# Parameter rows ahead of the first weights, and another order around the second half scan, in a kernel of two fused blocks

## The chip, the cores and the metric

The kernel runs on one core of a Trainium2 chip. The metric is the device time of one execution in microseconds (us): the median of the runs that are shown. A profiled execution has a span besides, from its first to its last instruction, which is a little shorter than its device time.

## What is computed

Two independent blocks read 2048 x 448 inputs in bfloat16, and their outputs stand side by side.

```python
# part A: a diagonal state space layer with 448 complex states
Lam_bar = exp(dt * Lam); B_bar = ((Lam_bar - 1) / Lam)[:, None] * Bmat
h[t] = Lam_bar * h[t-1] + B_bar @ x[t]              # t = 0 .. 2047
y = 2 * Re(h @ Cmat.T) + x * Dskip
# part B: attention of 16 heads of width 28, over 8 keys at distances 0, 2, .. 14
q, k, v = split(x @ wqkv); logits[s, w] = q[s] . k[s - 2w] / sqrt(28)
out = concat_heads(softmax_w(logits) @ v[s - 2w]) @ wo
```

## The kernel before

The order of TensorE (PE), VectorE (DVE), ScalarE (ACT) and SyncE (SP) is written out by hand in `plan`: each engine does its instructions in the order in which the lines issue them. GpSimd (POOL) is outside that list, with its own fixed order. Generators (`fill`, `vp`, `pv`, `sb`) hand out small pieces of long jobs, and `run(gen, n)` issues the next n of them; this is how independent work of one part is put between dependent steps of the other.

**Loads.** Two queues issue the transfers, those of SP and of ACT. ACT's has `load_w(1)` (the key weights, 336 KB, L115) and then three small parameter rows (`load_params`, L388, 1.8 KB each). SP's has the transposing loads of the first chunk of x (L106, L108), with `load_w(0)` (the query weights, L115) between the two, then the last 64 rows of the weights (`load_wt`, L119), and then the rest.

**Start.** TensorE runs matmuls on zeros (`warm`, L68 and L71) until data are there. `params` transposes the parameter rows on TensorE (`pt_p`, L441); ScalarE and VectorE make the step widths from them (L443 to L458), and `tables` goes on with three long VectorE instructions (L486, L488, L489) and sines on ScalarE. In VectorE's order these stand ahead of part B's first products.

**GpSimd at the start.** After short constants it copies weight columns into `wt` (`tail_w`, L124, two copies: one needs both `load_w`, the other `load_wt`). Then come memsets, and `consts` builds masks with affine selects: five of L159, L167, five of L161, L171, L175; after these thirteen come two memsets of `ones` (L163, L164), and more selects (L178).

**Part B.** For each of four chunks of 512 positions TensorE projects q and k (L194), ScalarE evicts them (L83), VectorE multiplies q with shifted k (`prod`, L240, and `prod_t`, L246), and TensorE adds up over the channels of a head with `ones` as weights (`sums`, L256, and L260, which needs the two memsets). `max_t` and `max_r` (L273, L279) find the largest logit, `max_s` subtracts it (L289) and takes the exponential. `norm` (L302 to L306) turns the weights and normalises them. `pv` (L322, L334) multiplies with v and adds, in pieces of VectorE; `turn` sends a finished group to a transposing DMA, `turn_p` does the last one on TensorE (L352), and `out` multiplies by wo (L362).

**Part A.** A time step is 16 p + 4 a + b: 128 values of p and 4 x 4 positions within. `local(b, m)` projects x for residue b and channel tile m (L595 to L603). The slots with b = 3 are joined over a, the carry over p is found by a scan, and everything is corrected with it. The scan runs in two halves, tiles 0 to 3 and 4 to 6: `last` (L620, L624, products L627 and L628), `rot` (L633, L634), `scan` (VectorE, L640 to L644), `back` (TensorE L633 and L634, copy by ScalarE L649). Then `groups(m)` finishes the slots of a tile (three matmuls L656, an addition on VectorE L658), `correct(b, m)` the other residues (two matmuls and a copy by ScalarE, or one matmul and an addition on VectorE, L673), and `y` gives the output (L689, L692). `groups(m)` for m of 4 to 6 needs the second half's `back`; `correct` of b = 0 and 1 needs `groups` of the same tile.

Of the kernel before, what the change touches and what calls it, by code (L numbers as in the profile page):

```python
# [12 lines left out]
ALU = mybir.AluOpType  # L13
# [16 lines left out]
CH = 512  # L30
# [343 lines left out]
class PartA:  # L374
# [273 lines left out]
        self.rot(reg, 1)  # L648
        self.nc.scalar.copy(self.u3[:, m0:m1, 0, 1:1 + NCH], ps[:])  # L649

    def groups(self, ms):
        nc, M = self.nc, self.mats
        for m in ms:
            ps = self.cx.ps([NCH, 3, NCH], f32, "gt", "mm")
            for i, p_ in enumerate((4, 8, 12)):
                nc.tensor.matmul(ps[:, i:3], lhsT=M[p_][:, m, :], rhs=self.slots(m, 0, 3 - i), start=(i == 0),  # L656
                                 stop=(i == 2), skip_group_check=True)
            nc.vector.tensor_tensor(self.slots(m, 1, 4), ps[:], self.slots(m, 1, 4), op=ALU.add)  # L658

    def correct(self, b, add, ms):  # L660
        nc, cx = self.nc, self.cx
# [37 lines left out]
@with_exitstack  # L699
def body(ctx: ExitStack, tc: tile.TileContext, A_x, A_Lre, A_Lim, A_Bre, A_Bim, A_Cre, A_Cim, A_logdt, A_Dskip,  # L700
         B_x, B_wqkv, B_wo, out):
    nc = tc.nc
    pool = ctx.enter_context(tc.tile_pool(name="sb", bufs=1))
    psum = ctx.enter_context(tc.tile_pool(name="ps", bufs=1, space=bass.MemoryType.PSUM))
    out_v = out[0].rearrange("(p j) e -> p j e", j=T)
    cx = Ctx(tc, pool, psum)
    b = PartB(cx, B_x, B_wqkv, B_wo, out_v[:, :, D:2 * D])
    a = PartA(cx, A_x, A_Lre, A_Lim, A_Bre, A_Bim, A_Cre, A_Cim, A_logdt, A_Dskip, out_v[:, :, 0:D])
    b.load_w(1, nc.scalar)
    a.load_params()  # L710
    b.load_x(0, (0,))
    b.load_w(0, nc.sync)
    b.load_x(0, (1,))
    b.load_wt()
    b.load_x(1)
    b.load_x(2)
    b.load_x(3)
    a.load_b()
    a.load_skip()
    b.load_w(2, nc.sync)  # L720
    a.consts()
    b.alloc()
    b.tail_w()
    b.consts()
    ET = mybir.EngineType
    with tc.manual_schedule(engines={ET.PE, ET.DVE, ET.Activation, ET.SP}):
        plan(a, b, cx, pool)


def run(gen, n=1):  # L730
    for _ in range(n):
        next(gen, None)


def plan(a, b, cx, pool):
    nc, chain = cx.nc, itertools.chain
    nc.scalar.activation(a.tload[:], cx.wz[0:1, 0:1], ACT.Exp)
    cx.warm(16)
    cx.warm(12, "cols")
    cx.warm(3, cols=CH)  # L740
    a.params()
    cx.warm(4, cols=CH)

    def proj(c, gs=range(NG + 1)):
        for g in gs:
            for which in (1, 0)[g // NG:]:
                b.proj_t(c, g, which, "A")
                yield

    def vproj():  # L750
        for js, r0, r1 in (((0, 1, 2, 3, 15, 14, 13, 12), 10, 14), ((11, 10, 9, 8), 6, 10), ((7, 6, 5, 4), 0, 6)):
            for j in js:
                b.proj_v(j, "A")
                if j == js[-1]:
                    run(xl, {10: 8, 6: 2, 0: 2}[r0])
                    b.halo(b.vd, r0, r1)
                yield

    sb, vp, tb, xl = a.setup_b("A"), vproj(), a.tables(), a.load_x((0, 2, 1, 3))
    fill = chain(proj(1), proj(2), proj(3))  # L760
    run(tb)
    first = [(g, which) for which in (1, 0) for g in (0, 1)]
    for g, which in first:
        b.proj_m(0, g, which, range(3))
    for g, which in (first[0], first[2], first[1], first[3]):
        b.proj_m(0, g, which, [3])
        b.proj_e(0, g, which, "A")
    run(proj(0, (2, 3)), 3)
    pr = [None, None]
    for g in range(NG):  # L770
        for s in range(2):
            pr[s] = b.prod(0, s, g, g + 1)
            if g == 2 and s == 0:
                b.prod_t(0)
    run(fill, 2)
    run(tb)
    run(fill, 5)
    b.sums(0, 0, pr[0])
    run(fill, 1)
    b.sums(0, 1, pr[1])  # L780
    p = b.prod(1, 0)
    b.prod_t(1)
    run(xl, 4)
    b.vd = pool.tile([NCH, TJ, DH, H], bf16, name="vd", tag="vd")
    b.zero_halo(b.vd)
    run(fill, 2)
    run(tb)
    b.max_t(0)
    run(tb)
    b.max_r(0)  # L790
    run(fill, 4)
    b.sums(1, 0, p)
    b.max_s(0)
    p = b.prod(1, 1)
    run(fill, 3)
    b.sums(1, 1, p)
    p = b.prod(2, 0)
    a.skip()
    a.params_g()
    b.prod_t(2)  # L800
    run(fill, 2)
    b.max_t(1)
    b.max_r(1)
    run(fill, 2)
    b.sums(2, 0, p)
    run(vp, 2)
    b.max_s(1)
    p = b.prod(2, 1)
    run(vp, 1)
    b.sums(2, 1, p)  # L810
    p = b.prod(3, 0)
    b.prod_t(3)
    run(vp, 1)
    run(sb, 1)
    b.max_t(2)
    b.max_r(2)
    run(vp, 2)
    run(sb, 1)
    b.sums(3, 0, p)
    run(vp, 1)  # L820
    b.max_s(2)
    p = b.prod(3, 1)
    run(sb, 1)
    run(vp, 2)
    run(sb, 1)
    b.sums(3, 1, p)
    run(vp, 1)
    run(sb, 1)
    b.max_t(3)
    a.alloc()  # L830
    a.params_m([0], nc.vector)
    b.max_r(3)
    a.params_m([1, 2, 3, 4], nc.vector)
    def loc(*bm):
        for b_, m in bm:
            a.local(b_, m)

    run(vp, 1)
    run(sb, 7)
    loc((0, 0))  # L840
    b.max_s(3)
    run(vp, 1)
    loc((0, 1))
    for j in range(0, T, 3):
        b.norm(j)
        run(vp, 1)
    run(vp, 16)
    a.load_c()
    b.load_wo()
    pv = chain(b.pv(0, 4), b.pv(4, 8), b.pv(8, 12), b.pv(12, 14), b.pv(14, 16))  # L850
    loc((2, 0), (2, 1), (1, 0), (1, 1), (0, 2), (0, 3), (3, 0), (3, 1))
    loc(*((b_, m) for b_ in (2, 1, 3) for m in (2, 3)))
    a.skip_mats()
    run(pv, 18)
    a.setup_c()
    a.scan_alloc()
    r = a.regs("g3")
    loc((0, 4))
    a.last(r[0])
    loc((2, 4), (0, 5), (1, 4), (2, 5), (3, 4))  # L860
    r_ = a.regs("rot")
    a.rot(r_[0], 0)
    run(pv, 4)
    a.scan(r_[0])
    loc((0, 6), (1, 5), (2, 6), (3, 5), (1, 6), (3, 6))
    rb = a.regs("bak")
    a.back(rb[0])
    run(pv, 3)
    a.last(r[1])
    run(pv, 2)  # L870
    a.groups((0,))
    b.out(0)
    a.groups((1,))
    run(pv, 1)
    a.rot(r_[1], 0)
    a.groups((2,))
    a.scan(r_[1])
    b.out(2)
    a.correct(1, "A", (0,))
    a.groups((3,))  # L880
    a.correct(1, "A", (1, 2))
    a.back(rb[1])
    run(pv, 1)
    a.groups((4,))
    run(pv, 1)
    a.correct(1, "A", (3,))
    a.correct(0, "A", (0,))
    a.groups((5,))
    run(pv, 1)
    a.correct(0, "A", (1,))  # L890
    a.correct(1, "A", (4,))
    a.groups((6,))
    run(pv, 1)
    a.correct(0, "A", (2,))
    a.correct(1, "A", (5, 6))
    for a_ in range(4):
        a.y(a_, 3)
        a.correct(0, "A", (3 + a_,))
    run(pv, 12)
    for i, (a_, b_) in enumerate(((0, 1), (1, 1), (2, 1), (3, 1), (0, 0), (1, 0), (2, 0), (3, 0))):  # L900
        a.y(a_, b_)
        if i < NM:
            a.correct(2, "AV"[i % 2], (i,))
            run(pv, 1 + i // 4)
        if i in (3, 6):
            run(pv, 2)
            b.out(4 + 2 * (i // 6))
    run(pv, 60 - 18 - 4 - 3 - 2 - 5 - 12 - 14)
    a.y(0, 2)
    a.y(1, 2)  # L910
    b.out(8)
    b.out(10)
    a.y(2, 2)
    b.out(12)
    run(pv, 99)
    a.y(3, 2)
    b.out(14, True)
# [31 lines left out]
```

## Time and profile before

| | us |
|---|---|
| median of 4 runs | 148.37 (148.03 to 148.98) |
| the profiled execution, device time | 148.98 |
| its span | 147.3 |
| TensorE busy in the span | 137.2 (93%) |
| VectorE busy | 128.8 (87%) |
| ScalarE busy | 88.2 (60%) |
| GpSimd busy | 23.6 (16%) |
| last parameter row: issue to the end of the wait for it | 3.62, from 2.29 |
| `pt_p` (L441) starts | 6.04 |
| first product of part B (L240) starts | 11.24 |
| first half of the scan: copy by ScalarE (L649) | 90.51 |
| second half: copy by ScalarE (L649) | 99.42 |

The page gives for each engine the time in which it was executing, and the same as digits over 40 slices of the span. The chain of waits goes back from the last instruction, at each step to what released it. The waits say who waited for whom and how long. The timeline lists instructions with their start, their length, and in brackets the idle time of the engine before them with its cause. The windows give busy time and the clock that TensorE was granted, as a share of full speed, in a stretch.

### The profile page before, as it was taken

The numbers are of one execution on the slowest core, as the hardware profiler recorded it, in microseconds if no ns is written. First come the engines' busy times: TensorE is split into PE (matmuls) and PEld (weight loads), VectorE is DVE, ScalarE is ACT, GpSimd is POOL, SyncE is SP. The second block draws the span as 40 slices with busy tenths as digits, with TensorE's granted clock in tenths as the row PEclk, the third lists the DMA queues.
The fourth block names the chain that finished last, engine by engine and source line by source line (L and its number), as shares of the span: only waits on it lengthen the run. The fifth ranks groups of instructions, "written<-read, shape, count | busy, mean of one in ns | idle before, by whom it ended". The sixth has DMA issues, their size and how long they took to land.

```text
span 147.3 us, 2545 instructions
## 1 busy us (share of the span) xinstructions
PE 137.2 (93%) x910; PEld 72.3 (49%) x921; DVE 128.8 (87%) x178; ACT 88.2 (60%) x177; POOL 23.6 (16%) x65
## 2 busy tenths in 40 slices
PE   6799999998979999899999999967999999999990
PEld 5244434443546676544445445524555555555550
DVE  0299999999999969999999999997999997799811
ACT  2279986598494997364656554464755445445550
POOL 8279999200000110000000000000000000000000
PEclk9999999999999999999999999995999999999999
DMA  4999893222223252629942389410602128226322
GB/s 114 279 190 201 175 197 66 47 44 54 51 40 66 45 150 45 159 52 219 145 95 70 70 162 144 119 62 0 125 31 67 62 52 229 67 95 158 125 93 93
DMA packets 42298, 15.67 MB, mean 106 GB/s; under 512 B 34786, under 2 KB 41840, under 8 KB 42285
## 3 DMA queue, kind: packets, MB, share of 16 engines
q1 hardware_dynamic: 41822, 15.16, 47.2%
q10 hardware_dynamic: 463, 0.35, 1.0%
q8 instruction: 7, 0.11, 0.3%
q14 instruction: 6, 0.05, 0.1%
HBM read 3.62 MB, written 3.67 MB: 49 GB/s over the span
## 4 chain that ended last, share of the span: by engine, by line
PE 59%; DVE 30%; issue 4%; DMA 2%; ACT 1%; ACTq 1%; DVEq 0%
PE u_ps L595 15%; PE y_ps L692 14%; DVE pr L240 12%; PE wo_ps L362 7%; PE v_ps L220 4%; DVE mat L554 3%; DVE prt L246 2%; DMA prow<-in_A_Lambda_im_dram 2%; PE y_ps L689 2%; PE co L667 2%; PE co L671 2%; PE u_ps L598 2%; PE gt L656 2%; PE lg L256 2%; DVE attn L306 2%
## 5 line engine op out<-in xcount | busy, mean ns | idle before, releaser
L334 DVE TENSOR_TENSOR pvb<-pvb,pvt 128x1792 bf16<-128x1792 bf16 (+1 forms) x35 | 31.4, 897 | 0.1
L322 DVE TENSOR_TENSOR pvt<-attn,vd 128x1792 bf16<-128x1792 bf16 (+1 forms) x35 | 31.0, 896 | 0.0
L240 DVE TENSOR_TENSOR pr<-qT,kT 128x2048 bf16<-128x2048 bf16 (+1 forms) x12 | 27.1, 2301 | 0.0
L595 PE MATMUL u_ps<-xaT,Bcat 128*128 128x512 bf16 x109 | 26.6, 379 | 0.2
L692 PE MATMUL y_ps<-C,u 128*128 128x448 bf16 x112 | 23.8, 353 | 0.0
L194 PE MATMUL qk_ps<-xbT,wqkv_nat 128*128 128x512 bf16 x93 | 22.1, 379 | 0.2
L695 ACT CAST ya<-y_ps 128x448 bf16<-128x448 f32 x16 | 8.5, 532 | 15.8 <-PE y_ps L692 13.0
L603 ACT CAST u<-u_ps 128x512 bf16<-128x512 f32 x21 | 12.4, 588 | 8.2 <-PE u_ps L595 5.2
L595 PEld LDWEIGHTS <-Bcat 128*128 128x128 bf16 x112 | 10.8, 98 | 12.4
L220 PE MATMUL v_ps<-wqkv_nat,xbT 128*128 128x448 bf16 x64 | 14.5, 357 | 0.0
L194 PEld LDWEIGHTS <-wqkv_nat 128*128 128x128 bf16 x96 | 9.0, 98 | 10.3 <-issue 0.3
L692 PEld LDWEIGHTS <-u 128*128 128x128 bf16 x112 | 9.8, 98 | 7.3
L362 PE MATMUL wo_ps<-wo_p,oT 128*128 128x448 bf16 x64 | 13.3, 352 | 0.0
L675 ACT CAST u<-co 128x512 bf16<-128x512 f32 x18 | 10.3, 588 | 3.0 <-PE co L671 2.9
L83 ACT CAST kT<-qk_ps 128x512 bf16<-128x512 f32 (+3 forms) x23 | 10.7, 466 | 0.8 <-PE qk_ps L194 0.6
L369 ACT CAST yb<-wo_ps 128x448 bf16<-128x448 f32 x14 | 7.4, 532 | 5.4 <-PE wo_ps L362 5.3
L83 ACT CAST qT<-qk_ps 128x512 bf16<-128x512 f32 (+1 forms) x20 | 9.8, 503 | 0.6 <-PE qk_ps L194 0.4
L83 ACT CAST vd<-v_ps 128x448 bf16<-128x448 f32 x16 | 8.3, 545 | 2.0 <-PE v_ps L220 1.9
L220 PEld LDWEIGHTS <-xbT 128*128 128x128 bf16 x64 | 8.2, 148 | 2.6 <-issue 0.8
L362 PEld LDWEIGHTS <-oT 128*128 128x128 bf16 x64 | 6.2, 98 | 5.6
L256 PE MATMUL lg<-pr,ones 128*32 128x512 bf16 x96 | 6.6, 382 | 0.8 <-DVE pr L240 0.8
L601 ACT CAST u<-u_ps 128x512 bf16<-128x512 f32 x7 | 4.1, 585 | 5.0 <-PE u_ps L600 5.0
(166 smaller groups left out, 185.3 us busy)
## 6 DMA issues: line engine op xcount, KB each, us to landing
out_dram<-ya SPq DMA_DIRECT2D x16, 112.0 KB, 1.7
out_dram<-yb SPq DMA_DIRECT2D x7, 224.0 KB, 2.1
vd<-vd SPq DMA_DIRECT2D x2, 392.0 KB
wqkv_nat<-in_B_wqkv_dram SPq DMA_DIRECT2D x2, 336.0 KB
wo_p<-in_B_wo_dram SPq DMA_DIRECT2D x16, 42.0 KB, 2.0
vd<-vd SPq DMA_DIRECT2D x1, 588.0 KB
xaT<-in_A_x_dram SPq DMA_TRANSPOSE x32, 2.9
bX<-in_A_B_re_dram SPq DMA_DIRECT2D x1, 392.0 KB, 4.7
```

Of the source, the lines that this page charges most:

```text
L83: nc.scalar.copy(out, in_)
L194: self.nc.tensor.matmul(self.ps_t[g, which][:], lhsT=wv[:, k], rhs=self.xT[:, k, c * CH:(c + 1) * CH], start=(k == 0), stop=(k == KT - 1))
L220: nc.tensor.matmul(ps[:], lhsT=xv[:, k, j, :], rhs=self.wn[:, k, 2, :], start=(k == 0), stop=(k == KT - 1))
L240: self.nc.vector.tensor_tensor(pr[:, :, g0:g1, :], self.qT[:, c, g0:g1].unsqueeze(1).to_broadcast([NCH, 4, n, CH]), self.windows(self.kT[: ...
L256: nc.tensor.matmul(lg[NW * t:NW * (t + 1), :], lhsT=self.ones[:, g, win], rhs=pr[:, 3 - t, g, :], start=(s == 0 and g == 0), stop=False, s ...
L322: V.tensor_tensor(buf(w) if w else acc, self.at[:, w, j0:j1, :].unsqueeze(2).to_broadcast([NCH, n, DH, H]), self.vd[:, off:off + n], op=AL ...
L334: V.tensor_tensor(acc, acc, buf(w), op=ALU.add)
L362: nc.tensor.matmul(ps[:], lhsT=oT[:, NSL * (i // 2) + 3 * n + k, :], rhs=self.wo_p[:, KT * n + k, :], start=(k == 0), stop=(k == KT - 1))
L595: nc.tensor.matmul(ps4[:], lhsT=self.Bcat[:, k, m, :], rhs=self.xT[:, b, k], start=(k == 0), stop=(b % 2 == 0 and k == KT - 1))
L603: nc.scalar.copy(self.h[b][:, m, :], ps)
L675: nc.scalar.copy(h_, ps)
L692: nc.tensor.matmul(ps[:], lhsT=self.state(m, a, b), rhs=self.C[:, m, :], start=False, stop=(m == NM - 1), skip_group_check=True)
```

## The change

Five things move. No arithmetic is added or removed, but for two of the matmuls on zeros.

1. The three parameter rows are issued first on ACT's queue, and behind them both `load_w(1)` and `load_w(0)`; SP's queue loses `load_w(0)`, so what stood behind it moves up.
2. Of the matmuls on zeros, two stand ahead of `pt_p` and three behind it, where it was three and four.
3. One projection piece is issued ahead of `max_t(1)` where it was behind it, and one piece of v ahead of `sums(2, 1)` where it was later.
4. Two `local` pieces go into the loop over `norm`, where pieces of v were used up.
5. Around the second half scan: `out(0)` goes ahead of `last`; `groups(0)` and `groups(1)` stand together, `out(2)` ahead of `rot`, `groups(3)` ahead of the scan; four corrections fill the time of the scan and two that of ScalarE's copy; `groups` 4 to 6 stand together behind it, and seven corrections are put between the y pieces. The pieces of `pv` are dealt out anew; their number is the same.

`groups` gets an option that no caller uses.

```diff
-    def groups(self, ms):
+    def groups(self, ms, add="V"):
...
-    b.load_w(1, nc.scalar)
     a.load_params()
     b.load_x(0, (0,))
-    b.load_w(0, nc.sync)
+    b.load_w(1, nc.scalar)
+    b.load_w(0, nc.scalar)
     b.load_x(0, (1,))
...
-    cx.warm(3, cols=CH)
+    cx.warm(2, cols=CH)
     a.params()
-    cx.warm(4, cols=CH)
+    cx.warm(3, cols=CH)
...
-    run(fill, 2)
+    run(fill, 3)
     b.max_t(1)
     b.max_r(1)
-    run(fill, 2)
+    run(fill, 1)
     b.sums(2, 0, p)
     run(vp, 2)
     b.max_s(1)
     p = b.prod(2, 1)
-    run(vp, 1)
+    run(vp, 2)
     b.sums(2, 1, p)
...
     for j in range(0, T, 3):
         b.norm(j)
-        run(vp, 1)
+        if j in (9, 12):
+            loc(((2, 0), (2, 1))[j // 12])
+        else:
+            run(vp, 1)
...
-    loc((2, 0), (2, 1), (1, 0), (1, 1), (0, 2), (0, 3), (3, 0), (3, 1))
+    loc((1, 0), (1, 1), (0, 2), (0, 3), (3, 0), (3, 1))
...
     run(pv, 3)
+    b.out(0)
     a.last(r[1])
-    run(pv, 2)
-    a.groups((0,))
-    b.out(0)
-    a.groups((1,))
+    a.groups((0, 1))
     run(pv, 1)
+    b.out(2)
     a.rot(r_[1], 0)
+    run(pv, 1)
     a.groups((2,))
-    a.scan(r_[1])
-    b.out(2)
     a.correct(1, "A", (0,))
     a.groups((3,))
-    a.correct(1, "A", (1, 2))
+    a.scan(r_[1])
+    a.correct(1, "A", (1,))
+    a.correct(0, "A", (0, 1))
+    run(pv, 1)
     a.back(rb[1])
-    run(pv, 1)
-    a.groups((4,))
-    run(pv, 1)
-    a.correct(1, "A", (3,))
-    a.correct(0, "A", (0,))
-    a.groups((5,))
-    run(pv, 1)
-    a.correct(0, "A", (1,))
-    a.correct(1, "A", (4,))
-    a.groups((6,))
-    run(pv, 1)
+    a.correct(1, "A", (2, 3))
+    a.groups((4, 5, 6))
     a.correct(0, "A", (2,))
-    a.correct(1, "A", (5, 6))
+    run(pv, 3)
+    rest = [(1, 4), (1, 5), (1, 6), (0, 3), (0, 4), (0, 5), (0, 6)]
     for a_ in range(4):
         a.y(a_, 3)
-        a.correct(0, "A", (3 + a_,))
+        for b_, m in rest[2 * a_:2 * a_ + 2]:
+            a.correct(b_, "A", (m,))
     run(pv, 12)
...
         if i in (3, 6):
-            run(pv, 2)
+            run(pv, 3 - i // 6)
             b.out(4 + 2 * (i // 6))
-    run(pv, 60 - 18 - 4 - 3 - 2 - 5 - 12 - 14)
+    run(pv, 2)
```

More of the change, by code (lines that the diff above doesn't have):

```diff
@@ L654, in groups @@
             ps = self.cx.ps([NCH, 3, NCH], f32, "gt", "mm")
+            if add == "A":
+                nc.tensor.matmul(ps[:], lhsT=self.cx.ident[:], rhs=self.slots(m, 1, 4), start=True, stop=False,
+                                 skip_group_check=True)
             for i, p_ in enumerate((4, 8, 12)):
-                nc.tensor.matmul(ps[:, i:3], lhsT=M[p_][:, m, :], rhs=self.slots(m, 0, 3 - i), start=(i == 0),
-                                 stop=(i == 2), skip_group_check=True)
-            nc.vector.tensor_tensor(self.slots(m, 1, 4), ps[:], self.slots(m, 1, 4), op=ALU.add)
+                nc.tensor.matmul(ps[:, i:3], lhsT=M[p_][:, m, :], rhs=self.slots(m, 0, 3 - i),
+                                 start=(i == 0 and add == "V"), stop=(i == 2), skip_group_check=True)
+            if add == "V":
+                nc.vector.tensor_tensor(self.slots(m, 1, 4), ps[:], self.slots(m, 1, 4), op=ALU.add)
+            else:
+                nc.scalar.copy(self.slots(m, 1, 4), ps[:])
     def correct(self, b, add, ms):
@@ L739, in plan @@
     cx.warm(12, "cols")
+    cx.warm(2, cols=CH)
+    a.params()
     cx.warm(3, cols=CH)
-    a.params()
-    cx.warm(4, cols=CH)
     def proj(c, gs=range(NG + 1)):
@@ L845, in plan @@
         b.norm(j)
-        run(vp, 1)
+        if j in (9, 12):
+            loc(((2, 0), (2, 1))[j // 12])
+        else:
+            run(vp, 1)
     run(vp, 16)
```

## The prediction

> **What bounds it now.** I read the digits first: TensorE and VectorE both stand at 9 nearly throughout, so a small stretch of either can pass to the end. Then the chain of waits, which names who ends last in each stretch. It begins on the change's ground:
>
> ```profile
> 2.29 3.62 DMA prow<-in_A_Lambda_im_dram
> 6.04 0.18 PE pt_p L441
> ...
> 8.31 1.14 DVE trn L486
> ...
> 10.18 0.97 DVE fr L489
> 11.24 3.77 DVE pr L240 x4
> ...
> 42.02 0.83 PE lg L256 x12
> ```
>
> The start is bound by the last parameter row; then VectorE runs without a gap from 11.24 to 51.24; from 42.02 TensorE carries the chain up to the largest logits of chunk 3 (L279, 52.74, where VectorE waits 1.5). After that VectorE bounds, with few gaps. The waits show those around the second scan:
>
> ```profile
> PE bakB L633 <- DVE rt L643: 0.9, 1, 0.9
> ...
> PE gt L656 <- ACT u L649: 0.6, 1, 0.6
> ...
> DVE u L673 <- PE co L669: 1.8, 1, 1.8
> ```
>
> The last is at 126.22: TensorE, behind there, keeps VectorE waiting. The windows show TensorE's busy time in two stretches of 3.40 us (third column on) and, after the five engines, its clock:
>
> ```profile
> 96.60:100.00 3.40, 1.70 (x7) 0.53 (x6) 3.37 (x8) 1.99 (x4) 0.00 (x0) 1.00 0.19 67
> 100.00:103.40 3.40, 3.18 (x11) 1.61 (x12) 2.27 (x4) 1.17 (x2) 0.00 (x0) 0.51 0.00 0
> ```
>
> A stretch half idle (gaps of 0.95, 0.15 and 0.57) is followed by one at half clock, which loses 1.7 of work. That is where the 1.8 at 126.22 comes from.
>
> **GpSimd's timeline** is the view on which this forecast turns:
>
> ```profile
> 8.11 0.29 POOL L124 COPY wt<-wqkv_nat 128x128 bf16<-128x128 bf16 x1 [0.90 <-DMA wqkv_nat<-in_B_wqkv_dram]
> ...
> 8.31 1.13 DVE L486 TENSOR_TENSOR trn<-kvc,turn 128x931 f32<-128x931 f32 x1
> ...
> 18.42 1.32 POOL L175 TENSOR_SCALAR_AFFINE_SELECT IS<-IS 128x128 bf16<-128x128 bf16 x1
> ...
> 19.48 3.45 DVE L240 TENSOR_TENSOR pr<-qT,kT 128x6144 bf16<-128x6144 bf16 x1
> 19.81 0.13 POOL L163 MEMSET ones<- 64x48 bf16 x1
> 19.99 0.13 POOL L164 MEMSET ones<- 64x48 bf16 x1
> ...
> 20.04 0.44 PE L260 MATMUL lg<-prt,ones 128*32 128x256 bf16 x8
> 20.08 2.90 POOL L178 TENSOR_SCALAR_AFFINE_SELECT IS<-IS 128x16 bf16<-128x16 bf16 x1
> ```
>
> A select of 16 columns takes 0.19 when it passes at once and 2.90 beside the long product: it ends at 22.98, 0.06 after that product (22.92). The same holds all the way from 9.05: a select ends within 0.2 of the end of the VectorE instruction beside it, one at each end, two at three of the ends. Memsets are not held. The thirteen selects ahead of L163 need ten such ends (two pass at L486's, two at L488's, one at L489's, the other eight at seven ends of L240 and L246), and the last passes at 19.75, just after the long product has begun. TensorE needs both memsets at 20.04 and 20.13. There is no slack at all.
>
> **The change, part by part.**
>
> *Rows first.* The three issues on ACT's queue took 1.51 (1.29 to 2.80); ahead of `load_w(1)` they run from 0.80 to 2.3, and the last row, 3.1 behind its issue's end now (2.79 to 5.90), lands at 5.4 at the latest. The rows now also wait behind 336 KB in their queue, and the first landed 2.6 after its issue (1.95 to 4.52), so 4.9 is in reach. TensorE has two matmuls on zeros ahead (4.48, 4.71), so `pt_p` comes at 4.92 to 5.5 for 6.04: 0.5 to 1.1 earlier; I take 1.1. ScalarE and VectorE are idle there and follow: L486 starts at 7.2 for 8.31.
>
> The weights pay: `load_w(1)` is issued 1.5 later, `load_w(0)` 0.5 later (its issue ended at 2.80, now some 3.3; it landed 3.76 later, so at 7.1). The projections begin at 5.7 for 7.01 by the warm matmuls, at 6.6 if the key weights share the transfers with x; the first eviction at 10.02 then moves to 9.0 to 9.6. ScalarE's table load starts behind one more issue, at 3.4 instead of 2.83, and with its activation ends at 4.9; the output of `pt_p` at 5.1 hides this, and it costs up to 0.5 if that cover goes. SP's later transfers move up by 0.6; nothing on the chain waits for them. Gain at the first product: 1.0, at least 0.3.
>
> *GpSimd behind it.* `load_wt` is issued at 3.93 for 4.55 and took 3.5 to land: 7.4, or 8.05 if the transfers are as full as now. Today the second copy (8.11) got in 0.2 ahead of L486. Now L486 begins at 7.2, ahead of it. The trace shows no copy beside a long VectorE instruction: its cost lies between 0.29 (it passes) and L486's 1.13 and beyond; I take the latter, as the selects, the nearest rows, also read and write this memory. Then the copy ends at 8.4, the memsets behind it take 0.65 as now (8.40 to 9.05), and the first select starts at 9.1, as today, but now beside L489 (9.1 to 10.2): the ends of L486 and L488, where four passed, are gone. Nine pass until the long product, which starts at 18.5 instead of 19.48; four are left, three if two pass at another end. The ends that follow are the long product's (21.95), L246's (23.1), L499's (24.2) and L500's (24.8): the memsets are done at 24.4 or 25.0, and TensorE stands at L260, reached at 19.0. Against 20.04 that is 4.4 or 5.0 later; I take 4.7, and as bounds 3.3 (two left) and 0.
>
> The Trainium skill ("SBUF — State Buffer", section "Who interferes with whom") speaks against this change here: it says that a VectorE instruction with two inputs in this memory shuts out a GpSimd instruction that reads it, not one that only writes, for the whole instruction, whoever came first going ahead. L486 has two such inputs and the copy reads; by the rule the copy loses its race, and the sum is the one below; without it, rival 1.
>
> *After that stall* TensorE has been idle for over 5 us; by the row above, 3.4 us at half clock follow: 1.7 lost, bounds 0 and 3.4. TensorE's own waits of 0.37 (35.23) and 0.81 (42.02) are swallowed: −1.18. Part 3 puts a piece of v (four matmuls, 0.76) ahead of the last logits: +0.76. The second, a projection piece, only changes place. At L279 (52.74): 4.7 + 1.7 − 1.18 + 0.76 = **+6.0**. VectorE, ahead by its two product buffers at most, waits there and has nothing to hide it.
>
> *Parts 3 and 4 without a stall* cost nothing: VectorE's chain covers them. The two `local` pieces replace v pieces of about the same length in the loop over `norm`.
>
> *The second scan.* Times are of before, on VectorE. `out(0)` ahead of `last` puts 1.51 of TensorE ahead of L620; its result then comes at 91.55, just before VectorE reaches L627. With fewer `pv` pieces and additions ahead of it the scan starts at 96.40 for 96.92, and the rotated result is done at 98.0 instead of 98.55. TensorE waits 0.65 for an addition's buffer, 1.1 at `back`, and 0.3 between its two matmuls; the copy's 0.57 is covered by two corrections, and the seven later corrections lie between y pieces. Followed through, TensorE is 3.38 ahead at the last y of this loop, VectorE 0.62. Then the 1.84 at 126.22 goes, since VectorE is late there: −0.62 − 1.84 = −2.46, and with the tail on TensorE, now freed from it, **−3.05** at the end if the clock holds. But idle time is 2.05 in 3.4, more than in the stretch above that was followed by half clock: then 1.7 goes again, −1.3. I take −2.2, between the two, as the idle may fall across two stretches. The option on `groups` costs nothing.
>
> The Trainium skill ("TensorE: Matmul & The Clock Gate", section "Why this matters for your kernels") asks only that gaps stay under about 3 us; by it the clock holds and the end is −3.05. The windows above, with no gap over 0.95 and a clock of 0.51 behind them, do not agree.
>
> **Sum.** 148.98 + 6.0 − 2.2 = 152.8 in the profiled execution (span 147.3 and 1.7 around it), which is 0.6 above the median of 148.37: **152.2**.
>
> **Rivals.**
> 1. *The selects keep up.* The copy gets in ahead of L486, or passes beside it, or the rows land no earlier than now so that nothing moves. For it: the copy and the selects are timed roughly, and `load_wt` is issued earlier. Against it: 7.4 is after 7.2. Then the start gives 0.3 to 1.0 and the middle 1.3 to 3.05: 148.37 − 1.6 to − 4.05, so 144.3 to 146.8; central 145.3, faster. The point that decides is whether the copy starts before L486.
> 2. *A short slip.* One or two selects are late, and the clock stays: 3.3 − 1.18 + 0.76 = +2.9 less 2.2 to 3.05, or less slip: 147.8 to 149.5.
> 3. *The forecast with the bounds of the clock:* 0 to 3.4 after the stall and 1.3 to 3.05 in the middle give 150 to 154.4.
>
> **Chances.** Forecast with its bounds (3) 0.56; rival 1 0.34; rival 2 0.10. The likeliest case's own range is 150 to 154.4; to hold 8 in 10 the range must reach over most of rival 1: 144.8 to 154.2. A measurement of this kernel can tell about 0.5% from no change, 147.6 to 149.1. Faster: rival 1 and a little of 2, 0.35; same: 0.06; slower: 0.59.
>
> **What would show it.** Right: `pt_p` near 4.9, L486 near 7.2, the second copy (L124) ending behind L486, L163 and L164 at 24 to 25, a wait of TensorE at L260 for GpSimd of some 5, half clock behind it, the wait at L279 up to 7; later no wait at L656 for ScalarE, and none of 1.8 at L673. Wrong: the copy ahead of L486, or selects that end away from VectorE's ends; then the sum is rival 1's.

## The result and the profile after

The changed kernel takes 147.48 us in the median (146.79 to 152.0) for 148.39 before (147.62 to 152.34): a ratio of 0.9934, with an interval of 0.9914 to 0.9953. It is **faster by 0.7%**: little, but the whole interval lies below 1. The forecast was 152.2, slower. Executions that are over 1.5% longer than the shortest of their kernel are left out of every ratio, which is why a median and a ratio can disagree below (e7, e16).

The profiled execution of the changed kernel is one of the longer ones: 149.86 us, span 148.2. A second profile, of an execution nearer to the median (e1: 148.1 us, span 146.4), is read beside it.

The first, in the timeline: start, length, engine, and in brackets the idle time before and its cause.

```profile
5.45 0.20 PE L441 MATMUL pt_p<-ident,prow 21*128 21x21 bf16 x1
...
7.02 1.47 PE L194 MATMUL qk_ps<-xbT,wqkv_nat 128*128 128x512 bf16 x6 [0.62 <-DMA wqkv_nat<-in_B_wqkv_dram]
...
7.56 1.13 DVE L486 TENSOR_TENSOR trn<-kvc,turn 128x931 f32<-128x931 f32 x1
...
9.37 2.12 PE L194 MATMUL qk_ps<-xbT,wqkv_nat 128*128 128x512 bf16 x9 [0.88 <-DMA wqkv_nat<-in_B_wqkv_dram]
...
9.46 1.67 POOL L124 COPY wt<-wqkv_nat 128x384 bf16<-128x384 bf16 x2 [5.35 <-DMA wqkv_nat<-in_B_wqkv_dram]
...
11.78 1.77 POOL L159 TENSOR_SCALAR_AFFINE_SELECT ones<-ones 128x16 bf16<-128x16 bf16 x5
12.26 5.92 DVE L240 TENSOR_TENSOR pr<-qT,kT 128x2048 bf16<-128x2048 bf16 x5 [1.73 <-ACT qT L83]
...
20.60 3.49 POOL L175 TENSOR_SCALAR_AFFINE_SELECT IS<-IS 128x128 bf16<-128x128 bf16 x1
24.15 0.13 POOL L163 MEMSET ones<- 64x48 bf16 x1
...
24.34 0.48 PE L260 MATMUL lg<-prt,ones 128*32 128x256 bf16 x8 [3.06 <-POOL ones L163]
```

`pt_p` came earlier as forecast (5.45 for 6.04), and L486 with it (7.56 for 8.31). But TensorE, which never waited for its weights before, now does so twice, the second time until 9.37. The first product comes at 12.26, **1.02 later** than before, where 1.0 earlier was forecast. In this execution the last select met the long product (20.60 to 24.09), and TensorE stood 3.06 at L260.

In e1 the weights are late too, but the selects are not:

```profile
9.93 2.12 PE L194 MATMUL qk_ps<-xbT,wqkv_nat 128*128 128x512 bf16 x9 [0.86 <-DMA wqkv_nat<-in_B_wqkv_dram]
...
11.57 0.78 POOL L159 TENSOR_SCALAR_AFFINE_SELECT ones<-ones 128x16 bf16<-128x16 bf16 x5
...
12.61 2.78 POOL L161 TENSOR_SCALAR_AFFINE_SELECT ones<-ones 128x16 bf16<-128x16 bf16 x5
12.83 6.01 DVE L240 TENSOR_TENSOR pr<-qT,kT 128x2048 bf16<-128x2048 bf16 x5 [2.52 <-POOL ones L161]
...
17.86 0.13 POOL L163 MEMSET ones<- 64x48 bf16 x1
```

VectorE sat idle 2.52 ahead of the first product, and five selects passed in 0.78, one every 0.15. The memsets are done at 18, well ahead of L260. (The product's wait is put down to GpSimd's select; ScalarE's eviction, which comes after the late weights, ended beside it.)

Around the second scan, two views of the profile of the changed kernel: the waits, and the windows as in the prediction.

```profile
PE bakB L633 <- DVE rt L643: 1.4, 1, 1.4
...
DVE u L662 <- PE gt L659: 0.7, 1, 0.7
```

```profile
97.70:101.10 3.40, 3.04 (x17) 1.41 (x16) 3.40 (x6) 2.47 (x5) 0.00 (x0) 1.00 0.28 96
101.10:104.50 3.40, 2.15 (x13) 1.21 (x14) 2.69 (x6) 1.78 (x4) 0.00 (x0) 1.00 0.00 0
```

One long wait at `back` is left, and 0.7 at the additions; the waits at the group products for ScalarE (0.6) and at L673 (1.8) are gone. Where the profile of before had 0.51, the clock is 1.00. (From `groups` on, the changed kernel has higher line numbers: its L659 and L662 are the matmul of L656 and the addition of L658 before.)

**A ruler.** In every profile I took three numbers: the start of the first product (L240), the start of L279 of chunk 3, and the end of the span. The middle difference is 41.1 to 41.5 wherever no select is late (three profiles with a late one have 44.55 to 46.22), so the kernel falls into two parts that add up. "Half" marks a stretch of 3.4 us at half clock in the last part; the profile of e5 has one in the first part, from 8.27 to 11.68. The span is given to 0.1, so the last column is good to 0.05.

| kernel | median | ratio (interval) | first product | to L279 | L279 to end |
|---|---|---|---|---|---|
| before | 148.39 | | 11.24 | 41.50 | 94.56 half |
| changed | 147.48 | 0.9934 (0.9914, 0.9953) | 12.26 | 44.55 | 91.39 |
| e1 changed again | 147.60 | 0.9930 (0.9898, 0.9961) | 12.83 | 41.47 | 92.10 |
| e2 points 1, 2 | 150.45 | 1.0075 (1.0031, 1.0120) | 12.68 | 41.48 | 93.14 |
| e3 points 3, 4, 5 | 146.49 | 0.9839 (0.9787, 0.9890) | 11.94 | 41.50 | 91.36 |
| e4 changed, masks first | 147.26 | 0.9912 (0.9877, 0.9946) | 12.14 | 41.48 | 92.98 |
| e5 changed, w0 on SP | 146.83 | 0.9889 (0.9834, 0.9944) | 13.85 | 41.47 | 91.38 |
| e6 e5, masks first | 147.20 | 0.9886 (0.9840, 0.9933) | 12.06 | 41.47 | 91.87 |
| e7 changed, w1 first on SP | 147.63 | 0.9808 (0.9731, 0.9885) | 11.33 | 41.51 | 91.36 |
| e8 e7, masks first | 146.07 | 0.9825 (0.9779, 0.9871) | 11.75 | 41.12 | 92.13 |
| e9 three more selects | 154.10 | 1.0328 (1.0267, 1.0389) | 11.78 | 46.22 | 94.50 half |
| e10 point 5 | 147.58 | 0.9907 (0.9875, 0.9940) | 11.86 | 41.50 | 92.44 |
| e11 points 3, 4 | 149.50 | 1.0016 (0.9973, 1.0059) | 12.00 | 41.49 | 94.51 half |
| e12 zeros in the gaps | 148.17 | 0.9968 (0.9940, 0.9997) | 11.52 | 41.50 | 93.18 |
| e13 points 3, 5 | 147.33 | 0.9903 (0.9864, 0.9942) | 12.12 | 41.49 | 92.39 |
| e14 points 4, 5 | 146.80 | 0.9862 (0.9817, 0.9906) | 12.13 | 41.49 | 91.58 |
| e15 e3 again | 146.66 | 0.9859 (0.9814, 0.9905) | 11.70 | 41.50 | 92.30 |
| e16 e7 again | 148.52 | 0.9832 (0.9771, 0.9893) | 11.37 | 46.13 | 91.40 |

Each run's ratio is against the kernel before on the same chip (medians there 148.57 to 149.07). Single profiles differ by up to 0.9 in the first column: 11.24 for before, 11.52 to 12.13 for the same start in e3 and e9 to e15. The mean of these nine is 11.81, and the profile of before is the earliest. In the last column, e1, e4, e6, e8 and e10 hold a wait of VectorE at L322 for a transfer of v (0.33, 1.51, 0.12, 0.64 and 0.51); why it differs is not shown.

### The profile page after: what moved, and what is told of

The parts are those of the page before. It is cut to its first block, busy times and chain, and to the rows that moved or that the text cites. A ratio compares the mean times of both kernels' runs of the same rounds, so it can differ in the third digit from the quotient of the medians.

```text
span 148.2 us, 2540 instructions
## 1 busy us (share of the span) xinstructions
PE 135.8 (92%) x908; PEld 71.4 (48%) x919; DVE 128.5 (87%) x178; ACT 88.2 (60%) x177; POOL 23.0 (16%) x65
## 4 chain that ended last, share of the span: by engine, by line
PE 35%; DVE 29%; issue 3%; ACT 0%
PE y_ps L698 14%; DVE pvt L322 7%; DVE pvb L334 7%; PE wo_ps L362 6%; PE v_ps L220 4%; DVE mat L554 3%; PE y_ps L695 2%; DVE attn L306 2%; PE co L673 2%; PE lg L256 2%; PE co L677 2%; DVE gsc L640 2%; DVE pvb L322 1%; DVE rec L305 1%; DVE u L662 1%
## 5 line engine op out<-in xcount | busy, mean ns | idle before, releaser
L322 DVE TENSOR_TENSOR pvt<-attn,vd 128x1792 bf16<-128x1792 bf16 (+1 forms) x35 | 30.9, 896 | 0.0
L240 DVE TENSOR_TENSOR pr<-qT,kT 128x2048 bf16<-128x2048 bf16 (+1 forms) x12 | 27.2, 2308 | 1.8 <-ACT qT L83 1.7
L246 DVE TENSOR_TENSOR prt<-qT,kT 128x2048 bf16<-128x2048 bf16 x4 | 4.9, 1222 | 3.0 <-PE lg L265 3.0
```

Of the source, the lines that this page charges most:

```text
L240: self.nc.vector.tensor_tensor(pr[:, :, g0:g1, :], self.qT[:, c, g0:g1].unsqueeze(1).to_broadcast([NCH, 4, n, CH]), self.windows(self.kT[: ...
L322: V.tensor_tensor(buf(w) if w else acc, self.at[:, w, j0:j1, :].unsqueeze(2).to_broadcast([NCH, n, DH, H]), self.vd[:, off:off + n], op=AL ...
```

## The experiments

**Front and rest apart: e1, e2, e3.** e1 is the changed kernel itself. e2 is before with the first two hunks of the plan alone, e3 is the changed kernel with these undone:

```diff
-    b.load_w(1, nc.scalar)
     a.load_params()
     b.load_x(0, (0,))
-    b.load_w(0, nc.sync)
+    b.load_w(1, nc.scalar)
+    b.load_w(0, nc.scalar)
...
-    cx.warm(3, cols=CH)
+    cx.warm(2, cols=CH)
     a.params()
-    cx.warm(4, cols=CH)
+    cx.warm(3, cols=CH)
```

> The changed kernel once more, for a second profile. Theory (the start loses, the middle gains): the profile shown of it took 149.86 us, 2.4 above its median, and L279 of chunk 3 came at 56.81 for 52.74 there; in an execution near the median of 147.5 it comes near 54.5, with L163 and L164 still after 23, and the rest is 3.2 shorter than before. Rival (the start is neutral in most executions): L279 near 52.7, L163 near 20, and the rest is only 0.9 shorter.

> The kernel before with points 1 and 2 of the change alone (rows first, weights on ScalarE's queue, two and three matmuls on zeros). Theory: the start loses, so 150.1 to 150.7 us against 148.4. Rival (neutral start): 147.9 to 148.5.

> The changed kernel with points 1 and 2 undone; points 3 to 5 stay. Theory: the middle alone gains some 3.2, so 145.2 us. Rival: the middle gives 0.9, so 147.5.

L279 came at 54.30 in e1, as the theory had it, though L163 was at 17.86, not after 23: the loss of the start is the late weights alone. The front alone costs 0.75%, 1.1 us, a little under the 1.7 expected; its first product is 1.4 later than in the profile of before, and L279 too (54.16 for 52.74); against the mean of 11.81 it is 0.9 later. Without the front the change gains 1.6%, 2.4 us (e15: 1.4%). The two add up to the measured 0.7% within the intervals. The rival, a neutral start, is out.

**Do the selects cost anything? e4.**

```diff
-    b.tail_w()
     b.consts()
+    b.tail_w()
```

> The changed kernel with GpSimd's masks built ahead of its two copies into wt (consts before tail_w), so that the selects run while the weights are still on their way. Theory of the selects: they pass at 0.2 each, L163 and L164 are done by 8, TensorE doesn't wait at L260, and of the loss at the start only the later weights are left: 145.5 to 146.8 us. Rival (the loss is the weights' alone, the selects only follow them): 147.3 to 147.6, with a wait of the same size elsewhere ahead of L279.

L163 was done at 7.2, and the time stayed (0.9912 for 0.9930, intervals over each other), with the first product still at 12.14. So in most executions the selects cost nothing, and the loss is the weights': my theory fell here, the rival held.

**Why are the weights late? e5 to e8.** The rows stay first in all four. e5 puts `load_w(0)` back on SyncE's queue; e7 puts `load_w(1)` first there and leaves `load_w(0)` on ScalarE's; e6 and e8 are these with the masks first.

```diff
+    b.load_w(1, nc.sync)
     a.load_params()
     b.load_x(0, (0,))
-    b.load_w(1, nc.scalar)
     b.load_w(0, nc.scalar)
```

> The changed kernel with load_w(0) put back on SyncE's queue, behind the first load of x as before; the rows stay first and load_w(1) second on ScalarE's. Theory of the order (the query weights were late because on ScalarE's queue they run beside the loads of chunk 1 of x, which SyncE then issues earlier): load_w(0) lands by 7.5 instead of 9.2 to 9.9, and the first product starts at 11.0 to 11.6 for 12.3 to 12.8. Rival (all is late because the first 336 KB are issued 1.3 later): it lands after 8.5, and the first product stays after 12. If the weights are in time the selects decide: by the step of the prediction L163 is done at 23 to 25 and the time is 148 to 150 us; if the selects keep up, 146.0 to 146.6.

> The same with GpSimd's masks built ahead of its copies. Theory of the order with the step of the selects: 146.0 to 146.6 us, 2 or more below the same without the masks first. If the selects don't matter: within 0.3 of it.

> The changed kernel with load_w(1) first on SyncE's queue, ahead of the first load of x, and load_w(0) on ScalarE's behind the rows: the engines that move data have work from the first issue on. Theory of the order: the key weights land by 4.5, the query weights by 7.5, the rows by 4.6, and the first product starts at 10.2 to 11.2; with the selects keeping up 145.4 to 146.4 us, with the selects late 148 to 150. Rival (issue time alone): the first x is 0.5 later and the gain is no more than 0.3 against 147.5.

> The same with GpSimd's masks built ahead of its copies: 145.4 to 146.4 us by the theory of the order, whatever the selects would do; within 0.3 of the same without the masks first if the selects don't matter.

The windows of one us each show what the transfers did; the last two columns are the share of the 16 engines that move data and the GB/s. The kernel before:

```profile
1.00:2.00 1.00, 0.74 (x8) 0.75 (x9) 0.20 (x1) 0.00 (x0) 0.97 (x5) 1.00 0.08 6
...
5.00:6.00 1.00, 0.30 (x2) 0.00 (x0) 0.00 (x0) 0.00 (x0) 0.00 (x0) 1.00 1.10 316
6.00:7.00 1.00, 0.96 (x5) 0.50 (x6) 0.51 (x4) 0.18 (x1) 0.30 (x1) 1.00 1.14 277
```

The changed kernel:

```profile
1.00:2.00 1.00, 0.74 (x8) 0.74 (x9) 0.20 (x1) 0.00 (x0) 0.97 (x5) 1.00 0.01 2
...
5.00:6.00 1.00, 1.00 (x5) 0.31 (x4) 0.11 (x2) 0.18 (x1) 0.00 (x0) 1.00 1.13 169
6.00:7.00 1.00, 0.40 (x2) 0.00 (x0) 0.90 (x8) 0.00 (x0) 0.00 (x0) 1.00 1.05 170
```

And e7:

```profile
5.00:6.00 1.00, 0.81 (x4) 0.40 (x5) 0.39 (x3) 0.18 (x1) 0.00 (x0) 1.00 1.11 306
6.00:7.00 1.00, 0.12 (x1) 0.00 (x0) 0.87 (x7) 0.00 (x0) 0.06 (x1) 1.00 1.31 306
```

In e5, where the two weights run beside each other, one on each queue:

```profile
5.00:6.00 1.00, 1.00 (x6) 0.30 (x4) 0.39 (x3) 0.18 (x1) 0.00 (x0) 1.00 0.98 329
```

Between 5 and 7 the engines are as busy in before, the changed kernel and e7, but in the changed kernel they move little more than half as much. Added up from 1 to 7 us, before moved 1.39 MB, the changed kernel 1.03 (e1 0.93), e5 1.19 and e7 1.39. Of the 0.36 MB that are missing only 0.04 are from 1 to 3, where the engines had little to do yet; 0.32 are from 3 to 7, where their shares add up to 4.46 for 4.69. So it is not the late issue alone that costs (the rival), but what the transfers run beside. The packets themselves show it too: the weights' packets of 896 B took 110 ns (5 to 6) and 88 ns (6 to 7) in the mean in the changed kernel, where transposing loads of x ran on the other queue; from 5 to 6 they took 48 before, 51 in e7 and 42 in e5, where x had hardly begun again. So two queues at once are not enough for the loss (e5 moved 329 GB/s); it came with the weights beside the loads of x.

Putting `load_w(0)` back (e5) doesn't mend the start, against my theory: its issue is where it was before, and the second wait goes, but both weights come at about 8, and the first product at 12.06 (e6) or 13.85 (e5, behind its 3.41 us at half clock). Putting `load_w(1)` first and alone does: in e7 the projections start at 7.15 and run without the second wait, and the gain (1.9%, on three executions) is the largest.

```profile
7.15 3.40 PE L194 MATMUL qk_ps<-xbT,wqkv_nat 128*128 128x512 bf16 x15 [1.03 <-DMA xbT<-in_B_x_dram]
```

Why the weights are slower beside the loads of x is not shown; that packets of the two queues take turns on the same engines would fit. The Trainium skill ("DMA: Bandwidth & Descriptors", section "Queues, rings and completion order") says that they do: each engine goes round the queues that have work. It gives no loss for it; here it was from some 300 to 170 GB/s. The expected 10.2 to 11.2 for e7's first product was missed by 0.1, since the first x now ended the wait.

e6 and e8 differ from e5 and e7 by 0.0 to 0.2%: masks first bring nothing on the executions that the ratio compares, and building them beside `params` holds VectorE up (from L445 to L486 it takes 2.6 in e8, 2.0 in e7). What they take away is a spread: of e7's and e16's twelve executions six took 149.2 to 151.1 and six 145.7 to 146.7; all six of e8 took 145.7 to 146.7.

**The slip itself: e9 and e16.** e9 is before with three selects doubled:

```diff
-            G.affine_select(out=oc, in_=oc, ..., base=DH - 1 - base, ...)
+            for _ in range(2 if g < 3 else 1):
+                G.affine_select(out=oc, in_=oc, ..., base=DH - 1 - base, ...)
```

> The kernel before, with three of GpSimd's selects on ones done twice, so that three more stand ahead of L163; nothing else moves, and the result of a repeated select is the same. This is the slip of the prediction by itself. By its step the three end with the long product (22.9), with L246 (24.1) and with L499 (25.1), the memsets are done at 25.3, TensorE waits 5.2 at L260, and the time is 148.4 + 5.2 - 1.2 = 152.4 us, with half clock behind the wait 154.1. Rival (the selects are not held so strictly, or VectorE's lead takes the wait up): below 150.4.

It took 154.1, the upper of the two numbers. In the timeline of e9 (L162 is the select, L257 one of the sums), and then in its windows, with the clock third from the end:

```profile
19.12 4.58 POOL L162 TENSOR_SCALAR_AFFINE_SELECT ones<-ones 128x16 bf16<-128x16 bf16 x3
...
23.61 0.88 PE L257 MATMUL lg<-pr,ones 128*32 128x512 bf16 x8 [2.87 <-POOL ones L162]
```

```profile
20.40:23.80 3.40, 0.53 (x8) 0.19 (x12) 3.10 (x1) 1.16 (x4) 3.34 (x3) 1.00 1.12 83
23.83:27.24 3.41, 3.19 (x27) 1.03 (x28) 0.00 (x0) 0.47 (x1) 2.56 (x12) 0.50 0.31 70
```

The three did not end at 22.9, 24.1 and 25.1: one was held by the long product, the last passed behind it. TensorE waited 0.47 and 2.87, half clock followed, and VectorE was idle 4.58 ahead of its next product, which begins as TensorE's L266 ends (28.09).

e16 was run to see whether an earlier start is worth anything once the weights are in time:

> The variant with load_w(1) first on SyncE's queue once more, on the same chip as the changed kernel without its front. Theory (an earlier start is worth its 0.4 once the weights are in time): 145.8 to 146.2 us, 0.3 to 0.6 below that kernel. Rival (the start is no longer worth anything): equal within 0.2. Where GpSimd's selects come late in an execution, 149 and more.

The profile fell on an execution of 150.57 us. Its timeline is the forecast's, step by step:

```profile
7.87 1.13 DVE L486 TENSOR_TENSOR trn<-kvc,turn 128x931 f32<-128x931 f32 x1
8.28 0.86 POOL L124 COPY wt<-wqkv_nat 128x128 bf16<-128x128 bf16 x1 [0.73 <-DMA wqkv_nat<-in_B_wqkv_dram]
...
19.74 3.46 POOL L175 TENSOR_SCALAR_AFFINE_SELECT IS<-IS 128x128 bf16<-128x128 bf16 x1
23.26 0.13 POOL L163 MEMSET ones<- 64x48 bf16 x1
...
23.45 0.53 PE L260 MATMUL lg<-prt,ones 128*32 128x256 bf16 x8 [3.06 <-POOL ones L163]
```

The copy comes behind L486's start and ends 0.15 behind its end (9.00); the last select meets the long product; TensorE waits 3.06, and half clock follows until 27.16. L279 is 4.66 later than in e7 (57.50 for 52.84), of which 3.06 are the wait; the other 1.6 are about what the clock takes (half of 3.4). One late select is enough. In e7's own profile the same kernel had L175 at 18.52, ahead of the long product, and no such wait. The executions without the slip are 0.3% below e15 (0.9832 for 0.9859), within the intervals: an earlier start is worth some 0.4 us, which these runs cannot tell from nothing.

**The order around the scan: e10, e11, e13, e14, e15.** Each is before with only the named points of the change, in the hunks of the diff above.

> The kernel before with point 5 of the change alone. Theory: the gain of the changed kernel without its front (146.5 for 148.4) is all from here, so 146.3 to 146.7 us. Rival (points 3 and 4 give part of it): 147 to 147.8.

> The kernel before with points 3 and 4 of the change alone. Theory (VectorE's chain covers them): 148.2 to 148.7 us. Rival: 147 to 147.8.

> Points 3 and 5 of the change, without the front and without point 4. Theory (the new scan order needs TensorE's lead at last, which point 4 gives: with point 5 alone VectorE waited 0.36 for L624 and 0.5 for a transfer of v): a wait at L627 as with point 5 alone, and 147.2 to 147.7 us. Rival (point 3, which brings a piece of v and so its transfer forward, gives the 1.0): 146.3 to 146.7, and no wait at L322 for a transfer.

> Points 4 and 5 of the change, without the front and without point 3. Theory: 146.3 to 146.8 us and no wait at L627. Rival (point 3 gives it): 147.2 to 147.7.

> Points 3 to 5 once more, beside the two: 146.4 us; it says how firm the 1.0 between this and point 5 alone is. If chips differ by that much, 147 to 147.6.

Points 3 and 4 alone bring nothing (e11). Point 5 alone brings 0.9%, not the 1.3% expected; with point 4 it brings 1.4%, with point 3 it doesn't get more. The waits of VectorE show why; e10, then e13, then e14:

```profile
DVE pvt L322 <- DMA vd<-vd: 0.5, 1, 0.5
DVE rt L627 <- PE g3B L624: 0.4, 1, 0.4
```

```profile
DVE rt L627 <- PE g3B L624: 1.0, 1, 1.0
```

```profile
DVE rt L627 <- PE g3B L624: 0.2, 1, 0.2
```

With `out(0)` ahead of it, L624 is too late for VectorE's L627 unless TensorE is ahead, and the two `local` pieces of point 4, done earlier, seem to give it that lead. The last column of the table follows these waits: 91.36 without one (e3), 92.39 with 1.0 (e13), 92.30 in e15, where `out(0)` itself waited 0.75 for a transfer, and 92.98 in e4, with 1.51 for v. The intervals of e13 and e14 overlap a little; the executions that they compare do not (147.0 to 147.7 and 146.5 to 146.9).

**The clock: e12.** Before, with the gaps filled:

```diff
     a.correct(1, "A", (1, 2))
+    cx.warm(4, cols=CH)
     a.back(rb[1])
+    cx.warm(2, cols=CH)
```

> The kernel before, with four matmuls on zeros ahead of the second back and two behind it, in TensorE's idle time there; the order stays. Theory of the clock (a part of the gain of the new order is that no stretch of 3.4 us at half clock follows the gaps, which happens in 12 of 28 executions of the kernel before and shows as a mean clock of 0.988): no such execution, and 147.7 to 148.3 us. Rival (the order alone gains): the same share of 0.988, and 148.4 to 149.

No execution of e12 has a mean clock of 0.988; of the kernel before, run beside it, 12 of 27 had (and one 0.977). One stretch of 3.41 at half clock is 0.988 of 147. The gain is 0.3%. Before takes 147.7 to 148.7 without such a stretch and 149.1 to 149.9 with one, so the executions of before fall into two heaps. Its median moves with the share of each (148.39 in the result, 148.57 to 149.07 beside the experiments), and the profiled execution (148.98) is of the upper. Of the changed kernel's executions, e1 among them, 5 of 48 have 0.989 or less.

## Why the prediction was wrong, step by step

- **Rows first** was right, half a us off: `pt_p` at 5.45 and 5.24 for 4.92, since the two matmuls on zeros ran up to 0.63 long, for 0.39 before; L486 at 7.56 and 7.34 for 7.2.
- **"The weights pay" is the step that failed first.** I let the query weights land at 7.1, as long behind their issue as before (3.76), and gave the first eviction 9.0 to 9.6. That took a transfer's time from a schedule in which it had the engines to itself. TensorE had them at 9.37 and 9.93, and the first eviction came at 11.09 and 11.65. The front's term is not -1.0 but +1.0 to +1.6 at the first product against the profile of before, +0.5 to +1.0 against the mean of 11.81; e2 puts it at 1.1 in time. It passes to the end undiminished (41.5 behind it).
- **The slip of the selects**, 4.7 and 1.7 for half clock behind it, is the step that gave the forecast its sign. It is a real mechanism with the forecast place (e16, e9), but the forecast made it the rule: e1 has 41.47 from the first product to L279, so there it cost nothing, and only 5 of the 48 executions took over 149, the profiled one with the slip among them. It failed where it took VectorE to be without a gap: the late weights left VectorE idle 1.7 to 2.5 ahead of the first product, and selects pass at 0.15 each there. And four boundaries were not needed: what is left behind the long product passes at once, as VectorE's next instruction (L246) waits for TensorE's L260. The wait is 3.06 in the two profiles that have it, not 4.7, and with the clock 4.66, not 6.4.
- **-1.18 and +0.76** for swallowed waits and the piece of v measured nothing: 41.5 from the first product to L279 with and without points 1 to 3, and with the slip 3.05 more (44.55), the whole wait.
- **The second scan** was right in mechanism and in size where the clock holds: -3.05 was worked out, and 94.56 became 91.36 to 91.40 (-3.2) in five of the ten profiles with points 3 to 5; the others, up to 92.98, have waits at L322 or L627. The half clock that was weighed in beside it (-2.2 taken) did not come: no profile of the new order has one there, though two stretches with TensorE busy for 2.0 (e1) and 2.15 of 3.4 were there. Against executions of the old order without half clock (93.14 in e2, 93.18 in e12) the new one is worth 1.8 where those waits are absent, less where they are not. The rule of the Trainium skill that the prediction weighed ("TensorE: Matmul & The Clock Gate") gave -3.05 here and was the better guide for the gap of 1.4; for before's own gaps (0.95 and 0.57) it is not, as e12 shows.
- **"Parts 3 and 4 cost nothing"** was right alone (e11), but with point 5 it was worth some 0.6 us more (e14 against e10 and e13).
- **The sum**: +6.0 at L279 measured +1.6 (e1), with the slip +4.1 (the profile above); -2.2 measured -2.5 (e1) and -3.2, of which 1.4 is the half clock that only some executions of before have. The bounds of rival 3, given as 150 and 154.4, come out of its own terms as 149.6 and 154.8.
- **Rival 1** had the right sign, and the selects do keep up in most executions, but not for its reason. The copies came behind L486, as the forecast had it (9.46 and 10.02 for 7.56 and 7.34), and the selects passed in VectorE's idle time; so the point that was to decide, whether the copy starts before L486, did not decide: in e7 and e16 the second copy starts 0.53 and 0.41 behind L486, and only e16 slipped. Its gain at the front wasn't there either.

e8 beats both kernels: 146.07, 1.75% below before, with all six executions within 1.0 us; its interval lies over those of e3 and e15, which keep the old start. e7 has the lowest ratio, at the price of the slip.

## What to carry to other kernels

A transfer that is moved behind others on another queue need not keep its landing time (7.1 was worked out here, 9.37 and 9.93 measured); add up the bytes that must arrive by each wait, and look at GB/s beside the share of busy engines, before pricing what an earlier small load frees. A race between an engine's free moments and a fixed list of small instructions was decided here by the idle time of the other engine, so a forecast of it must hold that idle time's error; with the list taken out of the race (masks first, e8) the spread went. And where the old kernel's executions fall into two heaps, compare like with like: of the 3.2 between two profiles around this scan, 1.4 was a clock that the old order lost in only some of its executions.

## What the runs showed of the hardware

- The same 16 engines moved 277 to 316 GB/s (share 1.10 to 1.14) in the kernel before, 329 (0.98) with the two weights on two queues (e5), and 169 to 170 (1.05 to 1.13) with the weights on one queue beside transposing loads of x on the other.
- A GpSimd select of 16 columns takes 0.19 beside an idle VectorE; beside the long product it took 2.90 before, and one of 128 columns 3.46 and 3.49.
- Half clock came after a stretch of 3.4 with TensorE busy for 1.70 (before), 1.56 (e5, 4.85 to 8.27) and 0.53 (e9), and not after 1.99 (e1) or 1.88 (e2). A wait of 3.06 lost the clock in e16, where it lies in one stretch (20.33 to 23.75, TensorE busy 0.36 of 3.42), and kept it in the profile of the changed kernel, where it is spread over two (2.28 busy of 3.60, then 1.71 of 3.50). The last of these is as idle as the stretch of before that was followed by half clock; what tells those two apart stays open.
